# Reordered first loads, K turned amid the first projections, second chunk's rows turned by DMA: an attention and gated-MLP block on one core

## The chip, the cores and the metric

One core of one Trainium2 chip. The metric is device time in microseconds (us), median of several executions. All runs here are fast ones; a program on one core has no slow die to compare with. What does scatter within one kernel, and matters below, is the TensorE clock in the first 14 us: the traces have it at full or at half rate ("the gate is open" or "closed" below). I go by the traces, where the same instruction of two kernels can be compared, and by the medians with their ranges. There is one trace for each kernel, and the head scatters: in four executions of one and the same head (before, chunk_only, fetch_early, best) the weight landed at 7.30, 7.16, 7.01 and 6.84 us and the first score matmul started at 11.71, 11.58, 11.43 and 11.52.

## The reference

A block with modulation from a conditioning vector: layer norm, grouped attention over a cache, then a gated MLP with a spatial mixing matrix. Only its first steps matter here:

```python
mod = (silu(c) @ w_mod).reshape(1, 6, 1, -1)      # six vectors of 512
h = layernorm(x) * (1 + ca) + sa                   # x is 2048 x 512
q = (h @ wq)                                       # 32 heads of 128; 8 groups of K, V
p = softmax(q k^T / sqrt(128)); o = p v            # 2048 keys
x = x + ga * (o @ wo)                              # then the MLP, untouched by the change
```

## The kernel before

Engines are ordered by hand. Before attention can start, one row tile of x is normalised, the modulation weight (`wmod_a`, 1 MB) is turned into columns by 32 one-column matmuls, the rows are turned on PE and modulated (`hT`), and 16 matmuls project the first 128 queries. `warm` fills PE's waits with matmuls on zeros, to keep its clock up.

```python
nc.scalar.dma_start(out=c_bf[:], in_=c_dram)
nc.sync.dma_start(out=x_sb[:, 0, :], in_=x_dram[:, 0, :])
nc.sync.dma_start(out=wmod_a[:], in_=wmod_dram[:, :, 0 : 2 * D])
k_nat = early.tile([P, SK], BF16, name="kT")
nc.sync.dma_start(out=k_nat[:, 0:HK]..., in_=k_rows)          # half of K, to be turned on PE
...
load_wq(0, nc.sync)
nc.sync.dma_start(out=x_sb[:, 1:CT, :], in_=x_dram[:, 1:CT, :])
...
warm(14)
xns0 = ln1_norm(0, 1, ln1_stats(0, 1))
mod_columns(0, wmod_a, 0)
ln1_turn(0, 1, xns0, on_act=(1, 3))
k_ps = bank("o_ps")[:].bitcast(BF16)
for kt in range(NKT // 2):
    nc.tensor.transpose(k_ps[:, kt * P : (kt + 1) * P], k_nat[:, kt * P : (kt + 1) * P], ident[:])
nc.scalar.copy(out=kT0[:, 0:HK], in_=k_ps)
warm(1)
...
for fn in qproj(0, list(range(REP)), 0, P, two_engines=True):  # 16 matmuls, then their copies
    fn()
warm(2)
```

Attention then runs in units of eight slots. Each slot issues two score matmuls, an exponential on ACT and eight matmuls with the values; other work is put into slots by `at(unit, slot, ...)` and `fill[unit, slot]`. The rows of chunk 1 (tiles 4 to 7) are prepared during unit 1, and the projections that read them fill slots from unit 2, slot 1 on:

```python
def ln1_at(ch, stats, norm, turn):
    st = {}
    at(*stats, lambda: st.update(r=ln1_stats(ch * CT, CT)))
    at(*norm, lambda: st.update(x=ln1_norm(ch * CT, CT, st["r"])))
    if ch == 1:
        at(*turn, lambda: ln1_turn(ch * CT, CT, st["x"]))     # 16 transposes on PE
    else:
        at(norm[0], norm[1] + 1, lambda: ln1_dma(ch * CT, CT, st["x"]))   # 4 DMA transposes
        at(*turn, lambda: ln1_dma_mod(ch))                    # modulation of the turned rows

ln1_at(1, (1, 1), (1, 5), (1, 7))
...
if b == 1:                                                    # in set_fill(b)
    it, slot = 2 + (2 + k) // 16, (1 + k // 2) % 8
```

## Time and profile before

| | kernel before |
|---|---|
| time, 3 runs | 1326.96 us (1326.68 to 1327.08) |
| span of the trace; PE busy; ACT busy | 1325.4 us; 98%; 81% |
| weight lands; projections start; first score matmul | 7.30; 9.56; 11.71 us |
| hole in the score matmuls at 27 us | 2.4 us |

PE is the chain almost throughout, so time can only be had where PE is idle or waits: before the first score matmul, and at the hole. The lines are in the prediction.

### The profile page before, as it was taken

Reading aid. Unit: us, or ns where it says so; the run is one execution under the profiler, and the core shown is the slowest. Engines: PE = TensorE matmul, PEld = TensorE weight load, DVE = VectorE, ACT = ScalarE, POOL = GpSimd, SP = SyncE. Lnnn points to the kernel's source line nnn. Section 1 sums busy time; section 2 is a strip of 40 time slices with the busy share of each in tenths; the row PEclk is TensorE's granted clock in tenths of the full one; section 3 lists DMA queues with packets and bytes.
Section 4 is the critical chain, followed back from the end, with each engine's and each line's share of the span. In section 5 each row is a group of like instructions: output and inputs, shape, how many; then the busy total and the mean of one; then the engine's idle time right before and its main releaser. Section 6 shows DMA issues by size and latency. Waiting matters only on the chain.

```text
span 1325.4 us, 27685 instructions
## 1 busy us (share of the span) xinstructions
PE 1302.4 (98%) x12142; PEld 859.2 (65%) x12349; DVE 473.3 (36%) x1166; ACT 1078.4 (81%) x1061; POOL 49.0 (4%) x92
## 2 busy tenths in 40 slices
PE   8999999999999999999999999999999999999997
PEld 5666666666666666666666666666666666644444
DVE  5532222222222222222222222222222566793444
ACT  6898999999999999999999999999999999650000
POOL 1200000000000000000000000000000000120000
PEclk9999999999999999999999999999999999999999
DMA  5451021102111111111110211021101121143300
GB/s 162 111 134 30 16 49 37 37 13 53 23 31 33 34 37 37 29 37 37 33 33 17 53 37 31 19 52 25 30 13 21 25 34 33 29 115 82 66 21 27
DMA packets 145984, 57.59 MB, mean 43 GB/s; under 512 B 136160, under 2 KB 141408, under 8 KB 145856
## 3 DMA queue, kind: packets, MB, share of 16 engines
q1 hardware_dynamic: 139200, 37.32, 14.4%
q0 software_dynamic: 4208, 16.39, 4.4%
q10 hardware_dynamic: 2448, 2.03, 0.6%
q8 instruction: 98, 1.61, 0.5%
q14 instruction: 30, 0.25, 0.1%
HBM read 21.37 MB, written 2.10 MB: 18 GB/s over the span
## 4 chain that ended last, share of the span: by engine, by line
PE 97%; issue 1%; DVE 1%; DMA 0%; POOL 0%; ACT 0%; SPq 0%; DVEq 0%
PE s_ps L928 35%; PE o_ps L950 35%; PE misc L885 7%; PE misc L1290 7%; PE misc L982 6%; PE s_ps L1136 2%; PE s_ps L1175 2%; PE o_ps L1311 1%; DMA wmod_a<-in_w_mod_dram 0%; PE s_ps L1311 0%; DVE bnst L691 0%; PE misc L833 0%; DVE xn L680 0%; PE misc L782 0%; PE misc L1052 0%
## 5 line engine op out<-in xcount | busy, mean ns | idle before, releaser
L935 ACT ACTIVATE pT<-s_ps 128x1024 bf16<-128x1024 f32 x1024 | 1044.5, 1024 | 84.3 <-PE s_ps L928 10.1
L950 PEld LDWEIGHTS <-pT 128*128 128x128 bf16 x8192 | 548.5, 98 | 241.2
L950 PE MATMUL o_ps<-v,pT 128*128 128x129 bf16 x8192 | 631.4, 220 | 0.0
L928 PE MATMUL s_ps<-qT,kT 128*128 128x512 bf16 x2048 | 609.0, 379 | 10.3 <-ACT qT L899 0.5
L961 DVE RECIPROCAL rall<-o_ps 128x2 f32<-128x2 f32 x256 | 43.7, 171 | 743.6 <-PE o_ps L950 743.3
L928 PEld LDWEIGHTS <-kT 128*128 128x128 bf16 x2048 | 199.2, 98 | 119.5 <-issue 1.2
L885 PE MATMUL misc<-hT,wq_g 128*128 128x512 bf16 (+2 forms) x482 | 167.8, 365 | 0.3 <-ACT hT L842 0.2
L982 PE MATMUL misc<-wo_g,oT 128*128 128x512 bf16 x385 | 145.9, 379 | 0.0
L962 DVE TENSOR_TENSOR onorm<-o_ps,rall 128x256 bf16<-128x256 f32 x256 | 108.7, 425 | 8.8
L1290 PE MATMUL misc<-wsp,z 128*128 128x512 bf16 (+2 forms) x555 | 100.5, 336 | 0.6 <-issue 0.3
L897 DVE CAST qT<-misc 128x512 bf16<-128x512 f32 (+1 forms) x128 | 86.9, 679 | 7.6 <-PE misc L885 7.5
L1290 PEld LDWEIGHTS <-z 128*128 128x128 bf16 x560 | 50.6, 98 | 48.5
L995 DVE TENSOR_TENSOR xacc<-misc,xacc 128x512 f32<-128x512 f32 x112 | 76.2, 680 | 0.0
L885 PEld LDWEIGHTS <-wq_g 128*128 128x128 bf16 x544 | 51.5, 98 | 1.5 <-DMA wq_g<-in_A_wq_dram 0.3
L982 PEld LDWEIGHTS <-oT 128*128 128x128 bf16 x512 | 50.1, 98 | 0.7
L1305 DVE TENSOR_TENSOR gb<-misc,bsp_bc 128x512 bf16<-128x512 f32 (+1 forms) x28 | 18.4, 658 | 58.3 <-PE misc L1290 58.3
L1136 PE MATMUL s_ps<-win_sb,hT 128*128 128x448 bf16 x128 | 27.0, 352 | 0.1
L1146 ACT ACTIVATE z<-s_ps 128x896 bf16<-128x896 f32 x16 | 14.7, 917 | 14.9 <-PE s_ps L1136 14.9
L1175 PE MATMUL s_ps<-hT,win_sb 128*128 128x512 bf16 x109 | 24.3, 379 | 0.2
L1183 ACT ACTIVATE z1T<-s_ps 128x1024 bf16<-128x1024 f32 x14 | 14.3, 1024 | 10.1 <-PE s_ps L1175 9.1
L691 DVE BATCH_NORM_STATS2 bnst<-x_sb 128x6 f32<-128x512 bf16 x32 | 21.8, 682 | 0.5
L706 POOL DMA_DIRECT2D wq_g<-in_A_wq_dram x7 | 5.3, 753 | 420.9 <-PE misc L885 420.9
(79 smaller groups left out, 279.5 us busy)
## 6 DMA issues: line engine op xcount, KB each, us to landing
wq_g<-in_A_wq_dram POOLq DMA_DIRECT2D x7, 512.0 KB, 3.9
v<-in_A_v_cache_dram POOLq DMA_DIRECT2D x7, 512.0 KB, 6.6
wo_g<-in_A_wo_dram POOLq DMA_DIRECT2D x7, 512.0 KB, 4.7
oT<-onorm SPq DMA_TRANSPOSE x128, 2.4
wsp<-in_w_mod_dram POOLq DMA_DIRECT2D x1, 2048.0 KB, 9.1
out_dram<-yout ACTq DMA_DIRECT2D x15, 128.0 KB, 1.7
win_sb<-in_B_w_in_dram POOLq DMA_DIRECT2D x1, 1792.0 KB, 9.4
x_sb<-in_A_x_dram SPq DMA_DIRECT2D x3, 512.0 KB, 5.5
```

The lines of the kernel that those rows point to most:

```text
L885: nc.tensor.matmul(ps[0][:, o0 : o0 + n], lhsT=wqs[g][:, dt, hh * DH : (hh + 1) * DH], rhs=hTs[ch][:, dt, c0 : c0 + n], start=(dt == 0), s ...
L897: nc.vector.tensor_copy(out=dst[:, 0:cut], in_=src[:, 0:cut])
L928: nc.tensor.matmul(s_ps[:, h * 512 : (h + 1) * 512].rearrange("p (r q) -> p r q", r=REP), lhsT=groups[g]["kT"][:, kt * P : (kt + 1) * P], ...
L935: nc.scalar.activation(out=pTs[u][:, 2 * i : 2 * i + 2, :], in_=s_ps[:].rearrange("p (k q) -> p k q", k=2), func=ACT.Exp, scale=inv_sqrt_dh,)
L950: nc.tensor.matmul(o_ps[:, hh % 2, 0 : DH + 1], lhsT=pTs[u][:, kt, hh * P : (hh + 1) * P], rhs=groups[g]["v1"][:, kt, 0 : DH + 1], start=( ...
L961: nc.vector.reciprocal(out=rall[:, c0 : c0 + 2], in_=o_ps[:, :, DH])
L962: nc.vector.tensor_tensor(out=onorms[u][:, hh - 1 : hh + 1, :], in0=o_ps[:, :, 0:DH], in1=rall[:, c0 : c0 + 2].unsqueeze(2).to_broadcast([ ...
L982: nc.tensor.matmul(X_ps[:], lhsT=oTs[u][:, hh, :], rhs=groups[g]["wo"][:, hh, :], start=(hh == 0), stop=(hh == REP - 1),)
L995: nc.vector.tensor_tensor(out=xaccs[j][:], in0=X_ps[:], in1=xaccs[j][:], op=ALU.add)
L1136: nc.tensor.matmul(ps[0][:, hf * 512 : hf * 512 + FC], lhsT=h2Ts[j // CT][:, dt, (j % CT) * P : (j % CT + 1) * P], rhs=win_sb[:, dt, FH + ...
L1175: nc.tensor.matmul(ps[0][:, k * 512 : (k + 1) * 512], lhsT=win_sb[:, dt, f * P : (f + 1) * P], rhs=h2Ts[2 * ch2 + k][:, dt, :], start=(dt ...
L1290: nc.tensor.matmul(g_ps[:, :n], lhsT=z2[:, st, f * P : (f + 1) * P], rhs=wsp[t][:, st, c0 : c0 + n], start=(st == 0), stop=(st == NT - 1 a ...
```

## The change

Its intent: the weight starts sooner and its first half is used sooner; the query weights no longer wait behind K; K's turn moves to where K has landed; and chunk 1 is turned by DMA as the later chunks are, so that PE is spared 16 transposes.

```diff
--- before.py
+++ after.py
@@ -694,10 +694,11 @@
 
     c_bf = res.tile([P, NDT], BF16, name="c_bf")
     nc.scalar.dma_start(out=c_bf[:], in_=c_dram)
-    nc.sync.dma_start(out=x_sb[:, 0, :], in_=x_dram[:, 0, :])
-    nc.sync.dma_start(out=wmod_a[:], in_=wmod_dram[:, :, 0 : 2 * D])
+    nc.scalar.dma_start(out=x_sb[:, 0, :], in_=x_dram[:, 0, :])
+    for i in range(2):
+        part = slice(i * D, (i + 1) * D)
+        nc.sync.dma_start(out=wmod_a[:, :, part], in_=wmod_dram[:, :, part])
     k_nat = early.tile([P, SK], BF16, name="kT")
-    nc.sync.dma_start(out=k_nat[:, 0:HK].rearrange("p (t d) -> p t d", d=DH), in_=k_rows)
 
     groups, wqs, hTs, qTs = {}, {}, {}, {}
 
@@ -732,6 +733,7 @@
     nc.gpsimd.memset(mhalf[:], -0.5)
     make_identity(nc, ident[:])
     load_wq(0, nc.sync)
+    nc.sync.dma_start(out=k_nat[:, 0:HK].rearrange("p (t d) -> p t d", d=DH), in_=k_rows)
     nc.sync.dma_start(out=x_sb[:, 1:CT, :], in_=x_dram[:, 1:CT, :])
 
     kT0 = early.tile([P, SK], BF16, name="kT")
@@ -858,17 +860,21 @@
         for dt in range(NDT):
             ln1_mod(hTs[ch][:, dt, :], hTs[ch][:, dt, :], dt)
 
-    warm(14)
+    warm(12)
     xns0 = ln1_norm(0, 1, ln1_stats(0, 1))
     mod_columns(0, wmod_a, 0)
     ln1_turn(0, 1, xns0, on_act=(1, 3))
-    k_ps = bank("o_ps")[:].bitcast(BF16)
-    for kt in range(NKT // 2):
-        nc.tensor.transpose(
-            k_ps[:, kt * P : (kt + 1) * P], k_nat[:, kt * P : (kt + 1) * P], ident[:]
-        )
-    nc.scalar.copy(out=kT0[:, 0:HK], in_=k_ps)
     warm(1)
+
+    def k_turn(half, copy):
+        k_ps = bank("o_ps")[:].bitcast(BF16)
+        kts = range(half * NKT // 4, (half + 1) * NKT // 4)
+        cols = slice(kts[0] * P, (kts[-1] + 1) * P)
+        for n, kt in enumerate(kts):
+            nc.tensor.transpose(
+                k_ps[:, n * P : (n + 1) * P], k_nat[:, kt * P : (kt + 1) * P], ident[:]
+            )
+        copy(out=kT0[:, cols], in_=k_ps[:, 0 : HK // 2])
 
     def qproj(b, heads, c0, n, two_engines=False):
 
@@ -900,9 +906,12 @@
 
         return [lambda hh=hh, dt=dt: mm(hh, dt) for hh in heads for dt in range(NDT)]
 
-    for fn in qproj(0, list(range(REP)), 0, P, two_engines=True):
+    for n, fn in enumerate(qproj(0, list(range(REP)), 0, P, two_engines=True)):
         fn()
-    warm(2)
+        if n == 2 * NDT - 1:
+            k_turn(0, nc.vector.tensor_copy)
+            k_turn(1, nc.scalar.copy)
+    warm(1)
     first = dict(r1=ln1_stats(1, 1))
     ln_stats(mv1, 2, x_sb[:, 2, :])
     first["x1"] = ln1_norm(1, 1, first["r1"])
@@ -1083,13 +1092,10 @@
         st = {}
         at(*stats, lambda: st.update(r=ln1_stats(ch * CT, CT)))
         at(*norm, lambda: st.update(x=ln1_norm(ch * CT, CT, st["r"])))
-        if ch == 1:
-            at(*turn, lambda: ln1_turn(ch * CT, CT, st["x"]))
-        else:
-            at(norm[0], norm[1] + 1, lambda: ln1_dma(ch * CT, CT, st["x"]))
-            at(*turn, lambda: ln1_dma_mod(ch))
-
-    ln1_at(1, (1, 1), (1, 5), (1, 7))
+        at(norm[0], norm[1] + 1, lambda: ln1_dma(ch * CT, CT, st["x"]))
+        at(*turn, lambda: ln1_dma_mod(ch))
+
+    ln1_at(1, (0, 7), (1, 2), (1, 7))
     ln1_at(2, (2, 4), (3, 1), (4, 5))
     ln1_at(3, (5, 1), (5, 5), (7, 4))
     rest_w = {}
```

## The prediction

> **What bounds the kernel now.** I read the page first: busy times, then the chain that ended last. TensorE (PE) is busy for 1302.4 of 1325.4 us, and the last chain is PE almost throughout.
>
> ```profile
> PE 97%; issue 1%; DVE 1%; DMA 0%; POOL 0%; ACT 0%; SPq 0%; DVEq 0%
> ```
>
> So nothing that runs beside PE can give much. What is left is the time in which PE has no work: 1325.4 - 1302.4 = 23.0 us in all, and every edit of the diff lies in the first 32 us. The table of stretches says how much idle PE time these hold: 12.00 - 8.61 = 3.4 us in 0 to 12, 0.5 us in 12 to 22, 0.8 us in 22 to 32 (9.52 and 9.16 of 10.00 busy). PE's fill-in matmuls (L766, on zeros) and its transposes count as busy there, so this is not yet the price of the head. For that I followed the chain of work from 0 to 13 us (start, length, what; both in us):
>
> ```profile
> 1.19 6.11 DMA wmod_a<-in_w_mod_dram
> 7.34 0.97 PE misc L782 x32
> 8.33 0.16 DVE modc L790
> 8.67 0.35 DVE hT L815
> 9.05 0.47 ACT hT L842
> 9.56 0.33 PE misc L885 x3
> 9.91 0.90 PE misc L885 x13
> 10.83 0.42 DVE qT L897
> ```
>
> The modulation weight lands at 7.30. Then 32 one-column matmuls, the columns' copies, the modulated rows hT (DVE and ACT take turns), the 16 first query projections and their copies follow one another. The first score matmul starts at 11.71. That is the whole serial head: until then attention, whose two matmul lines make 70% of the page's chain, cannot start.
>
> The DMA view of 0 to 10 us (40 slices of 0.25 us) shows when the engines really carry bytes, and how long issues take to land:
>
> ```profile
> GB/s 0 0 0 0 0 0 0 17 212 275 57 106 74 41 90 205 311 344 369 377 393 385 401 328 385 385 426 385 385 377 393 377 381 377 356 365 348 314 322 239
> wmod_a<-in_w_mod_dram SPq DMA_DIRECT2D x1, 1024.0 KB, 6.1
> wq_g<-in_A_wq_dram SPq DMA_DIRECT2D x1, 512.0 KB, 6.9
> ```
>
> The first hump (1.75 to 2.5) is the 128 KB of x. A trough follows, and full rate is reached only at 4.0 us. From there the queue is full: wmod, then K, then the query weights, the last landing at 2.57 + 6.9 = 9.5, just when the projections start.
>
> The second place is at 27 us, in the timeline by engine:
>
> ```profile
> 26.36 0.61 PE L950 MATMUL o_ps<-v,pT 128*128 128x129 bf16 x8
> 27.53 1.87 PE L833 MATMUL misc<-ident,xn 128*128 128x128 bf16 x16 [0.56 <-DVE xn L680]
> 29.23 0.59 PE L928 MATMUL s_ps<-qT,kT 128*128 128x512 bf16 x2
> ...
> 29.86 2.89 ACT L935 ACTIVATE pT<-s_ps 128x1024 bf16<-128x1024 f32 x3 [2.16 <-PE s_ps L928]
> ```
>
> Sixteen transposes of the second chunk's rows stand in PE's order before the next score matmul and wait for the normalised rows xn. Undisturbed, the score matmuls come every 0.88 us (25.01 and 25.93 are the last two starts), so that at 29.23 was due at about 26.81. The hole is 29.23 - 26.81 = 2.4 us, and ACT, next in line, sits idle for 2.16 us.
>
> **What the Trainium skill says.** "DMA: Bandwidth & Descriptors", section "Issuing engines are not separate DMA queues": issuing from another engine saves only the issuing time. The trace agrees in size: the x issue holds SP for 0.40 us and sends wmod from 0.73 back to 1.19. The section "Queues, rings and completion order" of that page has each engine consume one queue in ring order and take turns between queues by packets; so weights, query weights and K stay in the order of issue, and x on ACT's queue shares with wmod. The landings at 7.30, 8.01 and 9.49 fit the first half. "Perfetto Trace Analysis", section "DMA Optimizations", says that splitting lets part of the work start sooner, and also that small pieces cost rate: here the 1 KB rows of 14 to 19 us move at a mean of 348 GB/s, the 2 KB rows of wmod at 370 to 400 in the slices above. Splitting makes wmod's rows 1 KB. "TensorE: Matmul & The Clock Gate", Part 1, gives some 3.4 us of activity to full clock; the weight loads of the fill-in matmuls come every 0.43 us until 4.57 and then five come in 0.98 us, which agrees. Twelve instead of fourteen still pass that point.
>
> **The change part by part.**
>
> *Modulation weight earlier and in two parts.* Its issue moves from 1.19 to 0.73: 0.46 us. Against that stand 128 KB of x, now beside it instead of before it (0.35 us at 370 GB/s), and the lower rate of 1 KB rows (1 MB at 350 instead of 385: about 0.27 us). For it: the smaller first issue should fill the trough at 2.5 to 4.0 sooner, since two issues of 0.4 us replace one of 0.69; I guess 0.8 us of the 1.5 us trough. Sum: the second part lands near 6.6 instead of 7.3. The first part lands over a microsecond sooner, so half of the 32 column matmuls (0.48 of 0.97 us) leave the path. The columns are then 0.7 + 0.5 = 1.2 us earlier, and hT with them: 9.86 becomes 8.7.
>
> *Query weights before K.* They now follow the weight directly: 6.6 plus 512 KB at 350 GB/s, 1.5 us, makes 8.1 instead of 9.49. K follows, 256 KB at 380, 0.7 us: 8.8. They no longer bind, and hT sets the start of the projections. Without this part they would have eaten most of the first part's gain.
>
> *K turned amid the projections.* Before, its 8 transposes (0.61 us) ran in the wait for hT. Now they stand between the 8th and 9th projection, at about 9.1, where K (8.8) should just be there. They cost 0.61 us on the path. The copies split in two halves: about 0.5 us on DVE while PE finishes, about 0.6 us on ACT (256 columns took 0.37, 1024 took 1.01). Both end before the query copies.
>
> Head: the projections end at 8.7 + 0.9 + 0.6 = 10.2 to 10.3 instead of 10.81. Gain 0.5 us. The fill-in matmuls that go (three of 0.2 to 0.4 us) lie in waits and are worth nothing.
>
> *Second chunk by DMA.* The 16 transposes leave PE, and the statistics (4 pairs, 3.28 us on DVE) move up to where DVE is free, at 18.53. Without the head's shift: statistics end at 21.8; rstd takes 1.5 us more, as now (25.56 to 27.06); first row normalised at 23.74. Then four DMA transposes on SP's queue, each like these:
>
> ```profile
> 31.45 1.24 SPq L970 DMA_TRANSPOSE oT<-onorm  x1
> 80.60 1.37 DVE L815 TENSOR_SCALAR hT<-hT,modc 128x512 bf16<-128x512 bf16 x4
> ```
>
> The issue takes about 1.24 us, landing 2.4 us (page, median of the same shape). Issues at 23.8, 25.0, 26.3, 27.5; the last lands at 29.95. The modulation of four 512-column slices then takes 1.37 us, one every 0.32: 30.4, 30.7, 31.05, 31.4. PE would reach the first projection that reads hT about 2.3 us earlier than now, near 29.6; it has to wait for the slices instead, and its second matmul can start at 30.8 and end at 31.0. Now the score matmul after these two starts at 32.32. Gain 1.3 us, against 2.3 if the rows were there in time.
>
> Sum: 0.5 + 1.3 = 1.8 us. From there to the end the profile shows the same steady chain, so it arrives in full: 1326.96 - 1.8 = 1325.2 us.
>
> **The rivals.** (a) The rows land in time, since I overrate issue or landing by about a microsecond: then 2.3 + 0.5, 1324.2. For it: the queue is empty from 19 to 31 us (2 GB/s in 22 to 32). Against it: DVE also has casts between. (b) The DMA transposes are slower: the chunk after this one took 3.6 to 7.0 us from issue to landing, the next 6 to 15. For it: same tile and call. Against it: those ran beside a 2 MB load and several 512 KB loads, which are not there at 24 us. If the last lands at 32 all of 1.3 goes, and the onorm copies behind the modulation in DVE's order hold PE too: 1326.5 or worse. (c) The head gives nothing, because the 1 KB rows and x beside them bring wmod no earlier, or K is late and stops PE in the middle of the projections: 1326.96 - 1.3 = 1325.7. (d) The clock gate closes in the now longer sparse stretch before the projections: a few microseconds at half rate, 1 to 2 us lost. PE has work at 5 to 6 us that it hadn't, so I hold this for unlikely.
>
> **Range and chances.** The rivals lie between 1324.2 and 1326.7 and runs scatter by 0.2 us. Range 1323.8 to 1326.7. Two per cent would be 26.5 us; the diff touches 32 us, most of which is needed work. Within 2%: 0.99.
>
> **What would show it.** In the new trace: second weight part landing near 6.6 and query weights near 8.1; projections split by 8 K transposes with no wait before these; first score matmul near 11.2. Four transposes issued at about 23.3 to 27; the score gap at 27 us gone, with in its place a wait of about 1 us before the first projections of the next block, released by DVE. If that wait is missing, rival (a); if it is over 2 us, (b). If the first score matmul stays at 11.7, (c). The whole is wrong if the time falls by over 3 us or rises, since then something outside the first 32 us has moved.

## The result, and the profile after

| | before | after |
|---|---|---|
| median time (range) | 1326.97 us (1326.68 to 1327.08), 6 runs | 1327.68 us (1327.11 to 1328.23), 6 runs |
| span of the trace | 1325.4 | 1326.5 |
| weight, or its second part, lands | 7.30 | 7.58 |
| projections start | 9.56 | 9.44 |
| first score matmul | 11.71 | 12.97 |
| exponentials, start against before: first / 19th / last | | +1.25 / +0.86 / +0.86 |

The ratio after to before is 1.0005, interval 0.9993 to 1.0018. A ratio is the mean time of one kernel's runs over that of the other's of the same rounds, so it is not quite the ratio of the medians quoted here. The forecast gain of 1.8 us became, by the medians, a loss of 0.7: the head loses 1.25 us where it should have won 0.5, and the chunk wins 0.39 where it should have won 1.3. From the 19th exponential to the last the offset is the same, so nothing else moved.

The chain of work of the changed kernel from 0 to 14 us (start, length, what), the answer to the first chain in the prediction:

```profile
1.48 6.09 DMA wmod_a<-in_w_mod_dram
7.62 0.57 PE misc L784 x16
8.21 0.16 DVE modc L792
8.93 0.47 ACT hT L844
9.44 1.07 PE misc L891 x8
10.51 0.85 PE o_ps L874 x8
11.37 0.70 PE misc L891 x8
12.09 0.42 DVE qT L903
```

The second part lands at 7.58, later than the whole did before. That is not for want of bytes at the start; the DMA view of 0 to 10 us, to be set beside the one in the prediction:

```profile
GB/s 0 0 0 0 0 0 0 3 13 106 254 340 180 127 324 369 389 373 340 307 315 311 332 361 365 369 365 385 373 385 381 385 373 377 373 348 320 302 232 99
```

From 2.5 to 4.0 us (the 11th to the 16th slice) the engines move some 400 KB, where it was 143. The columns nevertheless end 0.12 us sooner, since 16 of 32 are already done. Then comes the loss: 16 projections and 8 transposes of K take 1.07 + 0.85 + 0.70 = 2.62 us, where the projections alone took 1.25. K itself (2.80 + 6.95 = 9.75) is not waited for. The same matmuls are slower, and the table of stretches from 9.0 to 12.5 us says why. First the kernel before, then the changed one; the column PEclk is the granted share of PE's clock.

```profile
core 0: us, PE busy (x) PEld busy (x) DVE busy (x) ACT busy (x) POOL busy (x), PEclk, DMA share, GB/s
9.00:12.50 3.50, 2.78 (x29) 1.77 (x28) 1.92 (x6) 2.24 (x5) 0.26 (x2) 1.00 1.27 253
```

```profile
9.00:12.50 3.50, 3.15 (x26) 2.59 (x26) 1.11 (x4) 1.35 (x3) 0.00 (x0) 0.61 1.34 213
```

The trace's clock record has PE at half rate from 8.32 to 11.74 us. My rival (d) is what happened.

At the second place the hole has gone from 27 us and a new one stands at 31, in the changed kernel's timeline:

```profile
24.90 6.09 SPq L857 DMA_TRANSPOSE hT<-xn  x4
30.36 0.61 PE L959 MATMUL o_ps<-v,pT 128*128 128x129 bf16 x8
32.64 0.70 PE L891 MATMUL misc<-hT,wq_g 128*128 128x512 bf16 x2 [1.67 <-DVE hT L817]
33.81 1.02 ACT L944 ACTIVATE pT<-s_ps 128x1024 bf16<-128x1024 f32 x1 [2.10 <-PE s_ps L937]
```

PE comes to the first projections of the next block, and the rows they read are not there: 1.67 us instead of the 1 us of the prediction. The two holes are alike, 2.16 us of idle ACT then and 2.10 now. The chain from 26 to 36 us leads from that wait back to a DMA:

```profile
28.86 3.23 DMA hT<-xn
32.18 0.42 DVE hT L817
```

The four transposes, issued at 24.90, 26.24, 27.55 and 28.86, land after 2.46, 2.42, 4.10 and 3.23 us. I had put 2.4 on each. Here is what else the DMA engines did from 23 to 33 us (40 slices of 0.25 us; then packets, MB and share of 16 engines by queue), and the second queue's line again for 29.5 to 30.6 us alone:

```profile
GB/s 0 0 0 0 0 0 0 0 0 0 0 0 63 223 207 31 0 23 215 215 72 0 1 180 217 119 71 0 123 218 143 10 10 22 0 0 0 0 0 0
q1 hardware_dynamic: 2176, 0.52, 33.2%
q8 instruction: 1, 0.02, 0.6%
```

```profile
q8 instruction: 1, 0.02, 5.4%
```

One 16 KB packet of instructions: 5.4% of 16 engines over 1.1 us is 0.95 us of one engine. It ran from 29.62 to 30.57, and both transposes that had packets in flight then were late. That pointed to an experiment.

### The profile page after: what moved, and what is told of

Same layout as the page of the kernel before. It is cut to its first block, busy times and chain, and to the rows that moved or that the text cites. A ratio compares the mean times of both kernels' runs of the same rounds, so it can differ in the third digit from the quotient of the medians. Undisturbed runs are those within 1.5% of the kernel's fastest.

```text
span 1326.5 us, 27868 instructions
## 1 busy us (share of the span) xinstructions
PE 1313.2 (99%) x12330; PEld 859.3 (65%) x12330; DVE 472.8 (36%) x1167; ACT 1077.1 (81%) x1061; POOL 48.8 (4%) x92
## 3 DMA queue, kind: packets, MB, share of 16 engines
q10 hardware_dynamic: 2592, 2.16, 0.6%
## 4 chain that ended last, share of the span: by engine, by line
PE 97%; DVE 1%; DMA 1%; SPq 0%; POOL 0%; issue 0%; ACT 0%; DVEq 0%
PE o_ps L959 35%; PE s_ps L937 33%; PE misc L991 8%; PE misc L891 8%; PE misc L1296 7%; PE s_ps L1142 2%; PE s_ps L1181 2%; PE o_ps L1317 1%; PE s_ps L1317 1%; DMA wmod_a<-in_w_mod_dram 0%; DMA hT<-xn 0%; DVE bnst L691 0%; SPq L857 0%; DVE hT L817 0%; DVE xn L680 0%; PE misc L1061 0%
## 5 line engine op out<-in xcount | busy, mean ns | idle before, releaser
L991 PE MATMUL misc<-wo_g,oT 128*128 128x512 bf16 x512 | 194.1, 379 | 0.0
L891 PE MATMUL misc<-hT,wq_g 128*128 128x512 bf16 (+2 forms) x544 | 191.7, 369 | 1.8 <-DVE hT L817 1.7
```

The source lines that it names most:

```text
L891: nc.tensor.matmul(ps[0][:, o0 : o0 + n], lhsT=wqs[g][:, dt, hh * DH : (hh + 1) * DH], rhs=hTs[ch][:, dt, c0 : c0 + n], start=(dt == 0), s ...
L991: nc.tensor.matmul(X_ps[:], lhsT=oTs[u][:, hh, :], rhs=groups[g]["wo"][:, hh, :], start=(hh == 0), stop=(hh == REP - 1),)
```

## The experiments

Theory A: the head of the change loses (K's transposes on the path, the clock gate), and the chunk part gains less than it could because PE meets the rows too early. Theory B: the chunk part is what costs. Each run's "before" is the median of the kernel before in the same job.

### The two halves of the change

**chunk_only.** The kernel before with the last hunk of the diff alone.

```diff
-        if ch == 1:
-            at(*turn, lambda: ln1_turn(ch * CT, CT, st["x"]))
-        else: ...
+        at(norm[0], norm[1] + 1, lambda: ln1_dma(ch * CT, CT, st["x"]))
+        at(*turn, lambda: ln1_dma_mod(ch))
-    ln1_at(1, (1, 1), (1, 5), (1, 7))
+    ln1_at(1, (0, 7), (1, 2), (1, 7))
```

> Head as before, only the second chunk's rows turned by DMA. Theory A (the head of the change loses 0.5 to 1.3 us, the chunk part gains a little): exponentials after the first 18 start about 0.4 us earlier than in the kernel before, time 1326.97 - 0.4 = 1326.6. Theory B (the chunk part is what costs, since DVE and PE now wait for the DMA): slower than before by 0.5 to 1 us, 1327.5 to 1328.

Measured 1326.65 us (1326.55 to 1326.86) against 1327.05. PE's wait before the projections is 1.85 us here; the third transpose again lands late, after 4.43 us. The chunk part gains 0.4 us: theory A.

**head_only.** The changed kernel with that hunk undone.

> Head of the change, second chunk turned on PE as before. Theory A: first score matmul at 12.2 to 13.0 us instead of 11.71 and nothing gained later, time 1327.4 to 1328.3. If the clock record shows no half-rate stretch in the head, 1327.4; if it shows one, 1328.2. Theory B: the head gains its 0.5 us, 1326.5.

Measured 1328.34 us (1327.50 to 1328.65) against 1327.05. First score matmul at 13.04 us, half rate from 9.81 to 13.22. The head costs over a microsecond; theory B has fallen.

### The head

**fill_gap.** The changed kernel with six fill-in matmuls between the two halves of the columns.

```diff
         for i in range(2):
+            if first == 0 and i == 1:
+                warm(6)
```

> The changed kernel with six more fill-in matmuls in PE's wait between the two halves of the modulation columns; no work leaves or joins the path. Theory A1 (the clock gate closed from 8.3 to 11.7 us because PE was too idle before): no half-rate stretch after 4.9 us, projections back to 0.07 us each, first score matmul about 0.8 us earlier than 12.97, time about 0.8 us below the changed kernel's 1327.7, 1326.9. Theory A2 (the half rate is chance and costs nothing of note; the delay is all late data): as the changed kernel, 1327.7.

Measured 1327.69 us (1326.90 to 1329.24) against 1327.05. In the trace the clock is full from 6.24 us on, projections and transposes take 1.70 us instead of 2.62, and the first score matmul comes at 12.36, 0.6 us sooner. But in that execution PE warmed up only at 6.24; the first twelve fill-ins ran at half rate until then, and the six behind them pushed the second half of the columns from 7.47, when their data was there, to 7.96. So the gate's price is shown (0.92 us on this stretch), but as a remedy the fill failed: the median did not move, and two of the five runs took 1329.2 us at the lower granted share (0.997).

**split_only.** The kernel before with the first edit alone.

```diff
-    nc.sync.dma_start(out=x_sb[:, 0, :], in_=x_dram[:, 0, :])
-    nc.sync.dma_start(out=wmod_a[:], in_=wmod_dram[:, :, 0 : 2 * D])
+    nc.scalar.dma_start(out=x_sb[:, 0, :], in_=x_dram[:, 0, :])
+    for i in range(2):
+        part = slice(i * D, (i + 1) * D)
+        nc.sync.dma_start(out=wmod_a[:, :, part], in_=wmod_dram[:, :, part])
```

> The kernel before with only the first edit: x on ACT's queue, modulation weight in two parts at once. K and query weights in their old order, K turned ahead of the projections, second chunk on PE. If the first edit gains nothing because the second part lands at 7.4 to 7.6 and the spared half of the columns (0.48 us) only makes up for it: columns end at 8.1 to 8.3 as before, query weights at 9.5 or later hold the projections, first score matmul 11.7 to 11.9, time 1326.9 to 1327.3 (1327.7 to 1328 if the clock gate closes). If it gains the 1.2 us of my prediction and K's and the query weights' order were the brake: columns end by 7.5.

Measured 1327.03 us (1326.87 to 1327.15) against 1327.00: nothing gained. The trace is more favourable than I expected: second part at 6.90, first score matmul at 11.16, the exponentials 0.55 us early to the last. The medians do not show it. Its chain from 0 to 12.5 us shows the new bound:

```profile
2.79 6.31 DMA wq_g<-in_A_wq_dram
9.15 1.11 PE misc L887 x16
```

The query weights, behind K, now hold the projections, as the change's second edit assumes.

**split_wq.** split_only with the query weights ahead of K; K still turned ahead of the projections.

```diff
     load_wq(0, nc.sync)
+    nc.sync.dma_start(out=k_nat[:, 0:HK]..., in_=k_rows)      # moved here from above
```

> The kernel before with the first edit and the query weights ahead of K, but K turned ahead of the projections as before. Tells why the second weight part landed at 6.90 with K next in the queue (one trace) and at 7.42 to 7.58 in the four traces with the query weights next. If the next load in the queue matters: second part at 7.4 to 7.6, K at 9.6 to 9.7, its transposes hold the projections until about 10.3, first score matmul 12.0 to 12.2, time 1327.3 to 1327.5. If 6.90 was chance: second part scatters, 6.8 to 7.6 with no order.

Measured 1327.49 us (1326.96 to 1328.62) against 1327.07. The second part landed at 6.88, so the next load in the queue does not explain 7.5. K landed at 9.04 and held its transposes (9.09) and so the projections (9.76); first score matmul 11.73, as before.

**k_amid.** The kernel before with the query weights ahead of K, K turned amid the projections, and 12 and 1 fill-ins; weight in one piece, chunk 1 on PE.

```diff
-    nc.sync.dma_start(out=k_nat[:, 0:HK]..., in_=k_rows)
...
     load_wq(0, nc.sync)
+    nc.sync.dma_start(out=k_nat[:, 0:HK]..., in_=k_rows)
-    warm(14)
+    warm(12)
-    (K's 8 transposes and their copy)
...
+        if n == 2 * NDT - 1:
+            k_turn(0, nc.vector.tensor_copy)
+            k_turn(1, nc.scalar.copy)
-    warm(2)
+    warm(1)
```

> The kernel before with only the query weights loaded ahead of K and K turned amid the projections (and 12 and 1 fill-in matmuls). If K's transposes, hidden before, now stand on the path: first score matmul 0.5 to 0.7 us later than 11.71, at full clock; time 1327.5 to 1327.7, near 1328.4 if the clock gate closes. If the placing is free: 1327.0.

Measured 1328.23 us (1327.65 to 1328.89) against 1326.99, and half rate from 9.98 to 13.39 us: the second case of the expectation. This part alone carries the head's loss.

**one_piece.** The changed kernel with the weight in one load.

```diff
-    for i in range(2):
-        part = slice(i * D, (i + 1) * D)
-        nc.sync.dma_start(out=wmod_a[:, :, part], in_=wmod_dram[:, :, part])
+    nc.sync.dma_start(out=wmod_a[:], in_=wmod_dram[:, :, 0 : 2 * D])
```

> The changed kernel with the modulation weight in one load again (2 KB rows), x still on ACT's queue, all else as changed. If the 1 KB rows and the second issue made the second part late (7.4 to 7.6 us in four traces of this head): the whole weight lands near 7.0. If x's bytes beside it and the slow first fill of the queue set the landing: again 7.4 to 7.6, and the columns, all 32 now after it, end about 0.5 us later than in the changed kernel, first score matmul 0.3 to 0.5 us later.

Measured 1327.73 us (1327.01 to 1328.27) against 1326.99; half rate for 6.83 us from 7.25. The whole weight landed at 7.15, 0.3 to 0.4 us before the second part in the other traces of this head, and the columns ended at 8.19, as in the changed kernel. In these traces what splitting spares and what it costs are equal. That the 2 KB rows are the reason is not shown: one load of such rows, in the head of the kernel before, landed anywhere from 6.84 to 7.30.

**x_first.** The changed kernel with x first on SP's queue.

```diff
-    nc.scalar.dma_start(out=x_sb[:, 0, :], in_=x_dram[:, 0, :])
+    nc.sync.dma_start(out=x_sb[:, 0, :], in_=x_dram[:, 0, :])
```

> The changed kernel with x back on SP's queue ahead of the two weight parts. If moving x beside the weight is what kept the second part from landing earlier (its 128 KB are carried while the weight's own packets could run): x lands near 3.0 instead of 4.7 to 5.8, second part no later than the changed kernel's 7.4 to 7.6 although issued 0.4 us later. If the issue time counts: second part at 7.9 to 8.0.

Measured 1328.19 us (1327.20 to 1328.52) against 1327.00. x landed at 2.98, the second part at 7.83: issued 0.44 us later, landed 0.25 to 0.4 later. In this one trace the issue time counts, nearly in full, and x beside the weight is not what delays it.

**after_14 and k_amid_14.** By now six of seven traces with 12 fill-ins had the half-rate stretch and none of seven with 14. These two restore the fill-ins and nothing else, in the changed kernel and in k_amid.

```diff
-    warm(12)
+    warm(14)
```

> The changed kernel with 14 fill-in matmuls at the start again instead of 12; they end before the second weight part lands, so the path is untouched. So far six of seven traces with the changed head (12 fill-ins, K turned amid) hold a half-rate stretch of 3.4 us or more that begins between 7.2 and 10 us, none of seven with 14 fill-ins does. If the two missing matmuls close the clock gate: no half-rate stretch in the head, projections and K's transposes together 1.7 us instead of 2.62, time 1327.0 to 1327.2 in most runs. If K's transposes amid the projections, or the phase of the window, do it: half rate again in most runs, 1327.5 to 1328.2.

> The K part alone (query weights ahead of K, K turned amid the projections) with 14 fill-in matmuls as before. If the missing matmuls close the gate: full rate, first score matmul 0.4 to 0.5 us later than in the kernel before, time 1327.4 to 1327.5. If not: 1328.2 again, as with 12.

Against 1327.03 in that job: after_14 1327.29 us (1326.63, 1326.99, 1327.29, 1328.75, 1328.77); k_amid_14 1327.35 us (four runs of 1327.22 to 1327.56, one of 1328.64), where k_amid with 12 had 1328.23. No half-rate stretch in either trace. after_14, chain from 0 to 14 us and stretch from 9.0 to 12.5:

```profile
9.18 0.33 PE misc L891 x3
9.53 0.44 PE misc L891 x5
9.97 0.45 PE o_ps L874 x8
10.41 0.46 PE misc L891 x8
```

```profile
9.00:12.50 3.50, 2.60 (x29) 1.84 (x29) 1.99 (x5) 1.52 (x5) 0.22 (x1) 1.00 1.31 242
```

So at full rate K's turn costs 0.45 us on the path (0.85 at half rate), and k_amid_14 loses 0.3 us by the median. Nine traces of 14 fill-ins are without the stretch, and six of seven with 12 have it (the seventh is fill_gap, with six more); k_amid's loss falls from 1.24 to 0.32 us when the two come back (in another job). So the two missing matmuls are what closes the gate in most executions. For the changed kernel alone the timed runs show less: medians 1327.68 and 1327.29, with ranges that overlap. Not in all, nor only they: the kernel before itself had 2 of 9 runs at 1328.2 in this job and 2 of 9 at 1328.4 to 1328.7 in the first, with the lower granted share (0.997) of the gated runs, and two runs of after_14 are of that kind. No trace of such a run of the kernel before was taken.

The traces also point to why so little decides. Their clock record opens at full rate at 3.84 to 7.18 us, depending on the execution, and in the six gated traces the half rate begins 3.41 us after that. In this stretch of 3.41 us PE was busy (`--windows`) for 1.45 to 2.16 us in the six, and for 2.03 to 3.21 us in the ten others. The lowest of the ten are chunk_only (2.03) and the kernel before (2.11); the changed kernel has 1.92, after_14 2.54. So how busy PE is in that stretch goes with the closing, and the kernel before stands near the edge. An exact threshold doesn't come out, since the two groups overlap by 0.13 us.

### The second chunk

**late_proj.** The changed kernel with the modulation of the turned rows and the next block's projections four slots later.

```diff
-    ln1_at(1, (0, 7), (1, 2), (1, 7))
+    ln1_at(1, (0, 7), (1, 2), (2, 3))
-                it, slot = 2 + (2 + k) // 16, (1 + k // 2) % 8
+                it, slot = 2 + (10 + k) // 16, (5 + k // 2) % 8
```

> The changed kernel with the modulation of the DMA-turned rows four slots later and the first projections of the next block four slots later, so that they do not meet a transpose still under way. If the chunk part's missing gain is PE's wait for these rows (1.67 us in the trace): the wait is gone and the time falls by 1.5 to 1.7 us, to 1326.1. If the wait only moves elsewhere (ACT or PSUM the next limit): less than 0.5 us gained.

Measured 1326.16 us (1325.19 to 1326.69) against 1327.05, 1.5 us below the changed kernel, although the half-rate stretch was there again (9.87 to 13.29). PE waits for no row any more.

**fetch_early.** chunk_only with one fill-in matmul in each of four slots replaced by 14 one-column ones, so that PE's instruction stream runs 104 ahead at the same time.

```diff
-        fill[0, i] = [lambda: warm(1)]
+        fill[0, i] = [lambda: tiny(14)]      # 128 x 1 instead of 128 x 512
```

> Second chunk by DMA alone (head as before), and in four slots of the first unit one 512-column fill-in matmul replaced by 14 one-column ones: 104 more PE instructions in about the same time, so that PE's instruction fetch of 16 KB (28.6 to 29.5 us in that trace) comes about 5 us sooner, before the transposes' packets. Theory F (the fetch holds one DMA engine, on which the third and fourth transposes wait): all four land 2.4 to 2.5 us after issue, the last by 30.0 instead of 30.94, PE's wait before the next block's projections shrinks by 0.8 to 1.0 us, time 1325.7 against 1326.65. Theory G (transposes in a row delay each other): third and fourth again 3.5 to 4.4 us, 1326.6.

Measured 1325.83 us (1325.69 to 1325.94) against 1326.99. The instruction packet now came at 22.40 to 23.28, before the transposes. These landed after 2.46, 2.42, 2.43 and 2.42 us, the last at 29.88. DMA view from 23 to 33 us, and PE's wait in the timeline:

```profile
GB/s 0 0 0 0 0 0 10 194 219 102 0 0 146 223 152 3 0 91 220 198 16 0 42 222 211 50 0 0 33 0 0 0 0 0 0 0 0 0 0 0
hT<-xn SPq DMA_TRANSPOSE x4, 2.4
```

```profile
30.37 0.70 PE L885 MATMUL misc<-hT,wq_g 128*128 128x512 bf16 x2 [0.87 <-DVE hT L815]
```

Four clean humps, and a wait of 0.87 instead of 1.85 us. Theory F holds: 0.8 us of the missing gain went to PE's own instruction fetch. The nine other traces with these four transposes agree: in each the packet ran while the third was in flight, the third took 4.07 to 4.43 us and the fourth 3.22 to 3.47. What is left, 0.87 us, is close to the 1 us that I had predicted for this wait, and the gain of this run, 1.16 us by the medians, is close to the 1.3.

**best.** Head as before, chunk by DMA, and late_proj's slots.

> Head as before, second chunk by DMA, modulation and next block's projections four slots later. The gains of the first job added: 1326.65 minus the 1.5 to 2.0 us that the later projections gave the changed kernel: 1324.7 to 1325.2, faster than both kernels in every run.

Measured 1324.90 us (1324.64 to 1326.14) against 1326.99; ratio 0.9988, interval 0.9974 to 1.0001. The exponentials start 0.19 us early at the first and 2.40 us at the last: the chunk part yields 2.2 us once nobody waits for the rows. The instruction packet still delays the third transpose (4.09 us), and it no longer matters. PE and ACT of its timeline:

```profile
32.58 0.62 PE L950 MATMUL o_ps<-v,pT 128*128 128x129 bf16 x8
33.03 0.59 PE L885 MATMUL misc<-hT,wq_g 128*128 128x512 bf16 x2
```

```profile
25.54 8.39 ACT L935 ACTIVATE pT<-s_ps 128x1024 bf16<-128x1024 f32 x9
```

No wait stands before the projections, and nine exponentials run without a gap.

**best_split.** best with split_only's edit.

> The fastest version so far with the first edit (x on ACT's queue, weight in two parts) added. If the first edit gains 0.3 to 0.5 us when it stands alone: 1324.4 to 1324.6 against 1324.9. If it is worth nothing, as the timed runs of it alone say: 1324.8 to 1325.0. Its trace shows a second time where the second part lands with K next in the queue: near 6.9, or 7.4 to 7.6.

Measured 1324.95 us (1324.71 to 1325.12) against 1327.07; ratio 0.9985, interval 0.9971 to 0.9998. The split adds nothing to best. Every run of it beats every run of both kernels; of best, the two slower runs (1326.01, 1326.14) still beat all of them. Either is the version to keep; best has fewer edits.

## Why the prediction was wrong

| step | predicted | changed kernel | after_14 |
|---|---|---|---|
| second weight part lands | 6.6 | 7.58 | 6.95 |
| query weights; K land | 8.1; 8.8 | 9.08; 9.75 | 8.41; 9.10 |
| projections end | 10.2 to 10.3 | 12.06 | 10.88 |
| first score matmul | 11.2 | 12.97 | 11.78 |
| gain of the head | 0.5 | -1.25 | -0.07 |

*Rival (d), "for unlikely".* This is the step that failed most. I argued that PE has work at 5 to 6 us that it hadn't, and counted neither the fill-ins taken away nor the waits between the small matmuls; and I wrote of the fill-ins that go that they "lie in waits and are worth nothing" and that twelve "still pass that point". They were worth the clock: 0.92 us in the changed kernel's trace, and 1.0 us between k_amid and k_amid_14, whose projections and transposes together take 2.72 and 1.69 us. The page "TensorE: Matmul & The Clock Gate", Part 1, which I had cited for warming up, also says that the gate looks at a free-running window of some 3.4 us, and the half-rate stretches here last 3.41 or 6.83 us. I used the half of the page about opening and not the half about closing.

*"I guess 0.8 us of the 1.5 us trough".* The start came about as I had hoped: the weight's first packets ran at 2.20 instead of 2.67 us, and the engines moved some 400 KB from 2.5 to 4.0 us instead of 143, although each half-size issue took 0.6 to 0.7 us, not 0.4. What I had wrong is the end, "lands near 6.6": each part ends with sixteen marks in the trace (packets of 4 bytes, one for each DMA engine as I read them), and it has landed only after the last. In the changed kernel's trace fourteen marks of the second part were done by 6.53, two only at 7.13 and 7.19, and it landed at 7.58. In after_14 fifteen were done by 6.24, the last at 6.59, and it landed at 6.95. With 12 fill-ins the second part landed at 7.42 to 7.58 in four traces, with 14 at 6.88 to 7.11 in four, which are of later jobs. Why some marks come late, and whether the fill-ins have to do with it, is open.

*"K ... should just be there".* Right: no wait. Its cost of 0.61 us was 0.45 at full rate. But even there the sum comes out at nothing (after_14, -0.07): in that trace the fill-ins, at half rate until 6.8, held the columns until 7.14, which the expectation of that run had ruled out, and K's turn took back what was left.

*The chunk.* The mechanism was right: PE waits for rows, released by DVE. The term "the last lands at 29.95" was mis-sized. Less the first score matmul's shift of 1.26, 32.09 is 30.83, 0.9 us late, and of this the instruction packet is the cause (fetch_early: 29.88). Rival (b) named slower transposes but blamed loads, which indeed weren't there; the page "Runtime: NRT & Kernel Launch", section "Instruction fetch mechanics", says that instructions come in 16 KiB blocks by DMA, and I had not looked there. The gain with the rows in time, put at 2.3 us, measured 2.2 (best).

*The sum.* Predicted -0.5 - 1.3. In the trace it is +1.25 - 0.39 = +0.86; by the medians +0.7. Of the head's miss of 1.75 us the closed gate made 0.92; the columns, ending at 8.19 instead of the 7.1 that the prediction comes to, made most of the rest. With the gate open the sum is about 0: after_14's exponentials are 0.23 us early at the last, its median 0.26 us above the kernel before. I had also written that a longer time would mean that "something outside the first 32 us has moved". It did not; the whole miss lies inside.

One reading was loose: the starts 25.01 and 25.93 are 0.92 us apart, not 0.88, and the hole is 2.4 us either way.

## What to carry to other kernels

Fill-in work on an engine whose clock depends on its activity is part of the path even where it lies in a wait; count it before taking it out, and look at the granted clock of the stretch. When work moves from an engine to DMA, see whether its consumer has to move too: the change gave 0.4 us with the reader where it was and 2.2 with the reader four slots later. DMA engines that carry no loads may still carry an instruction fetch: here one of 0.95 us delayed the kernel's own transposes and cost 0.8 us. And look at a load's last packets, not only at its rate: here two marks of sixteen came 0.6 us after the others.

## What the Trainium skill lacked or had wrong

- "Runtime: NRT & Kernel Launch", "Instruction fetch mechanics": calls the cost of crossing a 16 KiB boundary mostly hidden. That speaks of the engine that fetches. Here the cost fell on the kernel's own transfers: the fetch took 0.95 us of one DMA engine, and a transpose in flight landed after 4.1 instead of 2.4 us. The page doesn't tell of this, nor does "DMA: Bandwidth & Descriptors" ("Queues, rings and completion order"), which puts refills on row 14; the profile of the kernel before shows 98 instruction packets of 16 KB on queue 8, and smaller ones on queue 14.
- "TensorE: Matmul & The Clock Gate", Part 1: its rule is to leave no idle gap above some 3.4 us, and for shorter waits it gives no figure. In the changed kernel PE's longest wait in the head is 1.48 us, and the gate closed for 3.41 us all the same; PE had been busy for 1.92 of the 3.41 us before. With two fill-ins of 512 columns more, no trace here shows it.
- "DMA: Bandwidth & Descriptors", "DMA Transpose (X-bar)": no duration for a small transpose within SBUF. Here 128 x 512 bf16 took 1.2 us to issue and 2.42 to 2.46 us to land, four in a row 1.3 us apart without delaying each other.
- "Perfetto Trace Analysis", "DMA Optimizations": splitting may let work start sooner. Here it did (in the changed kernel's trace the first 16 columns ran at 5.60 instead of 7.34 us), but the work behind it waits for the last part, and the split alone left the time where it was: 1327.03 against 1327.00.
